# Feed-forward first product as seven block products for blocks 3 to 8, with streamed weights

## The chip, the cores and the metric

The kernel runs on one core of a Trainium2 chip. The metric is the device time of one execution in microseconds (us), taken as the median of several runs. The profiler's trace of one execution lists the instructions of the five engines: TensorE (PE; PEld is its weight load), VectorE (DVE), ScalarE (ACT), GpSimd (POOL) and SyncE (SP), on whose queue all DMAs of this kernel are issued.

## The reference

Three stages over 8 sequences of 576 tokens with 512 features; T = 4608 tokens in all.

```python
# 1 attention with landmarks, per head (8 heads of 64): A, Bm, C are softmax products with 32 means of q and k
out = A @ Z @ C @ v                     # Z: six steps of Z = 2 Z - Z Bm Z
# 2 feed-forward block
u = x + real(fft(fft(x, axis=1), axis=2))
un = (u - mean(u)) / sqrt(var(u) + 1e-6)
x = u + relu(un @ w_ch1) @ w_ch2        # w_ch1 512 x 2048, w_ch2 2048 x 512
# 3 gated block; x_prev is x moved by one token
k = relu((mu_k x + (1 - mu_k) x_prev) @ w_k)     # 512 x 1024
v = k * k @ w_v                                   # 1024 x 512
r = sigmoid((mu_r x + (1 - mu_r) x_prev) @ w_r)   # 512 x 512
return r * v
```

## The kernel before, in words

Every dense product is made with float16 halves. A float32 value is split into a high half and a low half, and a product is the sum of three matmuls (`PARTS`: high with high, high with low, low with high).

The program is recorded first and ordered afterwards. `Plan` collects every operation with a cost, and `issue()` is a list scheduler: on each engine it takes, among the operations that are ready in its own model of time, the one with the largest key. The key is the longest path of costs to the end (`tail`) plus the `lead` under which the operation was recorded: NOW 1000 for operations on the path of a feed-forward block, START 400 for the first sequence, SOON 200 for the later sequences, CONVERT 170 for the conversion of w_ch1 and w_ch2, 0 for the weights of stage 3. The order of each engine and of the SP queue is then fixed in the program. The matmuls of the feed-forward blocks and of stage 3 carry `chain=True`: they run in the order of recording, with a lead of 0, and everything else on TensorE (names with `gp`) goes between them. Where the plan sees TensorE idle for longer than some 0.45 us before the end of block 0 it puts matmuls on zeros into the gap (line 1142: `spare` before the first block, `acc<-zero` inside a block).

Stage 1 is `batch(b)`, once for each of 8 sequences. It leaves u in `ub`, three buffers of 512 tokens. Stage 2 runs over 9 blocks of 512 tokens (blocks 0 to 8): `norm(i)` (lines 1218 to 1285) makes the normalized operand `un`, and `block_a(i)` (lines 1287 to 1331) makes the two products. Its `first(f)`, one for each of 16 column groups of w_ch1, is 12 matmuls of 512 columns into a PSUM bank `ph`, then Relu on ACT and the low half on DVE into `h`. Its `second(f)` is 12 matmuls of 512 columns into the four banks `acc`. Firsts and seconds alternate, each second one step behind.

Weights arrive as 64-bit numbers whose bits the kernel converts itself. `Weights.run` loads a piece of 128 x 512 into a staging buffer, converts it with three operations on ACT and two on DVE, and leaves the two halves in SBUF. Of such pieces w_ch1 has 16 and w_ch2 has 16; both weights stay in SBUF (`w1`, `w2`) for all of stage 2. Staging buffers are two of `wst` and one inside `more`, which lies where the third `ub` buffer will be.

Stage 3 has already the form that the change brings to stage 2: its product with w_k is made in seven products of half-size blocks with matmuls of 256 columns (`Gated.first`, lines 1481 to 1543), with weight sums that `Weights.pair` (lines 576 to 588) makes in the background during blocks 1 to 3 of stage 2, writes to DRAM (`dw_k`) and loads again before stage 3.

Of the kernel before, what the change touches and what calls it, by code (L numbers as in the profile page):

```python
# [28 lines left out]
NB = T // BLK  # L29
HS = S // 2 + 1  # L30
# [112 lines left out]
NOW, START, CONVERT, SOON = 1000.0, 400.0, 170.0, 200.0  # L143
# [381 lines left out]
class Weights:  # L525
# [18 lines left out]
    def single(self, src, top):  # L544
# [3 lines left out]
        st = iss.tile(self.pool, [128, 2 * WCH + 2], I32, "wst", bufs=2)  # L548
# [14 lines left out]
    def pair(self, srcs, dram):  # L563


        iss = self.iss
        v_, s_, g_ = iss.v, iss.s, iss.g
        (a, e0), (b, e1) = [self.single(x, self.tops[0]) for x in srcs]
        h = WCH // 2
        u, w = slice(0, h), slice(h, WCH)  # L570
        s1, s2, s3, s4 = e0[:, u], e0[:, w], e1[:, u], e1[:, w]
        g_.tensor_tensor(s1, a[:, w], b[:, w], op=ALU.add)
        g_.tensor_tensor(s2, s1, a[:, u], op=ALU.subtract)
        g_.tensor_tensor(s3, a[:, u], a[:, w], op=ALU.subtract)
        g_.tensor_tensor(s4, b[:, u], s2, op=ALU.subtract)
        for x, at in ((a[:, u], 0), (b, 1), (e0, 3), (e1, 5)):
            n = wide(x) // h
            both = iss.tile(self.pool, [128, 2, n, h], F16, "wboth", "wtop1")
            xs = x.rearrange("p (n f) -> p n f", n=n)
            s_.activation(both[:, 0], xs, AF.Copy, scale=WS)  # L580
            v_.scalar_tensor_tensor(
                both[:, 1], xs, WS, both[:, 0], op0=ALU.mult, op1=ALU.subtract
            )
            iss.load(dram[:, :, at:at + n], both)

    def run(self, src, hi, lo, room=None):


        iss = self.iss
        v_, s_ = iss.v, iss.s  # L590
        if room is None:
            st = iss.tile(self.pool, [128, 2 * WCH + 2], I32, "wst", bufs=2)
            top = self.tops[self.count % 2 if hi is not None else 0]
            self.count += 1
        else:
            st, top = room
        iss.load(st.bitcast(U8)[:, 1:8 * WCH + 1], src.bitcast(U8))

        def words(dt, at):
            return st.bitcast(dt)[:, at:2 * WCH + at].rearrange("p (f w) -> p f w", w=2)[:, :, 0]  # L600

        x = words(F32, 2)
        byte = st.bitcast(I8)[:, 8:8 * WCH + 8].rearrange("p (f b) -> p f b", b=8)[:, :, 0]
        s_.activation(x, byte, AF.Prelu, bias=self.EDGE, alpha=self.STEEP)
        s_.activation(
            top.bitcast(I8).rearrange("p (f b) -> p f b", b=4)[:, :, 3], x, AF.Prelu,
            scale=8.0, bias=-8.0 * (56.0 + self.EDGE), alpha=1.0 / self.STEEP,
        )  # L610
        v_.scalar_tensor_tensor(
            words(I32, 1), words(I32, 1), 5, top,
            op0=ALU.logical_shift_right, op1=ALU.bitwise_or,
        )
        w = words(F32, 1)
        dram = None
        if hi is None:
            dram = lo
            both = iss.tile(self.pool, [128, 2, WCH], F16, "wboth", "wtop1")
            hi, lo = both[:, 0], both[:, 1]  # L620
        s_.activation(hi, w, AF.Copy, scale=WS)
        v_.scalar_tensor_tensor(lo, w, WS, hi, op0=ALU.mult, op1=ALU.subtract)
        if dram is not None:
            iss.load(dram, both)
# [465 lines left out]
def build(nc, tc, a):  # L1090
# [5 lines left out]
    with stack, tc.manual_schedule():  # L1096
# [51 lines left out]
        w1 = [iss.tile(pa, [128, 4, FF1], F16, f"w1{x}") for x in "hl"]  # L1148
        w2 = [iss.tile(pa, [128, 16, DM], F16, f"w2{x}") for x in "hl"]
        weights = Weights(iss, com)  # L1150

        def piece(name, rows, cols, parts, at):

            r, c = 128 * rows, WCH * cols
            sl = slice(c, c + WCH)
            return (
                a[name][r:r + 128, 2 * c:2 * c + 2 * WCH], parts[0][:, at, sl],
                parts[1][:, at, sl],
            )

        w12_items = []
        for g in range(4):
            w12_items += [piece("w_ch1", c, g, w1, c) for c in range(4)]
            w12_items += [piece("w_ch2", f, 0, w2, f) for f in range(4 * g, 4 * g + 4)]


        shapes = {"w_k": [128, 2, 7, 2, FF2 // 2], "w_v": [128, 2, 8, DM], "w_r": [128, 2, 4, DM]}
        kept = {
            n: iss.dram(tc.dram_tile(x, F16, name="d" + n), x, F16, "d" + n)
            for n, x in shapes.items()  # L1170
        }

        def far(name, rows, cols):
            r, c = 128 * rows, WCH * cols
            return (
                a[name][r:r + 128, 2 * c:2 * c + 2 * WCH], None,
                kept[name][:, :, rows, c:c + WCH],
            )

        def far_pair(name, c, g):  # L1180
            col = 2 * WCH * g
            h = WCH // 2
            return (
                [a[name][128 * r:128 * r + 128, col:col + 2 * WCH] for r in (c, c + 2)],
                kept[name][:, :, :, c, h * g:h * g + h],
# [3 lines left out]
        far_items = [far("w_v", f, 0) for f in range(8)] + [far("w_r", c, 0) for c in range(4)]  # L1189
# [28 lines left out]
        def norm(i):  # L1218
# [13 lines left out]
            uc = [iss.tile(pa, [128, BLK], F32, "uc", f"uc{c}") for c in range(4)]  # L1232
# [42 lines left out]
            rb = spread(r)  # L1275
            un = []
            for c in range(4):
                v_.scalar_tensor_tensor(uc[c], uc[c], 4.0, rb, op0=ALU.mult, op1=ALU.mult)
            iss.lead = NOW
            for c in range(4):  # L1280
                hi, lo = [iss.tile(pa, [128, BLK], F16, "un", f"un{x}{c}") for x in "hl"]
                s_.activation(hi, uc[c], AF.Copy)
                v_.tensor_tensor(lo, uc[c], hi, op=ALU.subtract)
# [3 lines left out]
        def block_a(i, un):  # L1287
            u = ub[i]
            acc = acc_banks()
            hs = {}  # L1290
            iss.lead = NOW

            def first(f):
                ps = ph()
                sl = slice(128 * f, 128 * f + 128)
                for c in range(4):
                    for n, (x, y) in enumerate(PARTS):
                        mm(
                            ps, w1[x][:, c, sl], un[c][y], c == 0 and n == 0,
                            c == 3 and n == 2, chain=True,  # L1300
                        )
                h = hs[f] = iss.tile(com, [128, 2, 512], F16, "h", bufs=3)
                s_.activation(h[:, 0], ps, AF.Relu)
                v_.scalar_tensor_tensor(
                    h[:, 1], ps, 0.0, h[:, 0], op0=ALU.max, op1=ALU.subtract
                )

            def second(f):
                h = hs.pop(f)
                for m in range(4):  # L1310
                    sl = slice(128 * m, 128 * m + 128)
                    for n, (x, y) in enumerate(PARTS):
                        op = mm(
                            acc[m], w2[x][:, f, sl], h[:, y], f == 0 and n == 0,
                            f == 15 and n == 2, chain=True,
# [372 lines left out]
```

## Time and profile before

| | us |
|---|---|
| median of 3 runs | 1493.27 (1493.11 to 1494.37) |
| the profiled execution, its own time | 1494.1 |
| its span from first to last instruction | 1492.3 |
| TensorE busy (share of the span) | 1476.0 (99%) |
| DVE, ACT, POOL busy | 906.2, 619.1, 341.6 |
| start of block 0 (first `ph` matmul) | 69.16 |
| start of stage 3 | 1028.3 |

The blocks of stage 2 start at about 69, 202, 320, 440, 550, 660, 770, 861 and 946 us. Until block 6 the matmuls of the sequences run between those of the blocks; from block 7 on the blocks run alone. Matmuls are pipelined in the engine, so that a duration of 379 ns for 512 columns is longer than the time from one to the next; the pace is read from the chain of waits, which gives the time of a run of matmuls.

### The profile page before, as it was taken

The numbers are of one execution on the slowest core, as the hardware profiler recorded it, in microseconds if no ns is written. First come the engines' busy times: TensorE is split into PE (matmuls) and PEld (weight loads), VectorE is DVE, ScalarE is ACT, GpSimd is POOL, SyncE is SP. The second block draws the span as 40 slices with busy tenths as digits, with TensorE's granted clock in tenths as the row PEclk, the third lists the DMA queues.
The fourth block names the chain that finished last, engine by engine and source line by source line (L and its number), as shares of the span: only waits on it lengthen the run. The fifth ranks groups of instructions, "written<-read, shape, count | busy, mean of one in ns | idle before, by whom it ended". The sixth has DMA issues, their size and how long they took to land.

```text
span 1492.3 us, 23013 instructions
## 1 busy us (share of the span) xinstructions
PE 1476.0 (99%) x9189; PEld 798.9 (54%) x9189; DVE 906.2 (61%) x1830; ACT 619.1 (41%) x1292; POOL 341.6 (23%) x398
## 2 busy tenths in 40 slices
PE   9999999999999999999999999999999999999998
PEld 5554455554554544545544444445656666666664
DVE  7877685766757646535435271212877788768762
ACT  4666544444354432322323131113455545554531
POOL 3002122132301201201202040000442435353410
PEclk9999999999999999999999999999999999999999
DMA  8353241232243311100005000001001001100100
GB/s 291 109 183 118 83 164 38 91 103 85 78 140 104 128 48 50 47 29 0 1 29 212 0 29 1 29 0 57 22 36 57 29 29 57 57 29 32 54 29 29
DMA packets 48987, 101.14 MB, mean 68 GB/s; under 512 B 4336, under 2 KB 14832, under 8 KB 48368
## 3 DMA queue, kind: packets, MB, share of 16 engines
q1 hardware_dynamic: 48880, 99.67, 19.6%
q8 instruction: 72, 1.18, 0.3%
q14 instruction: 35, 0.29, 0.1%
HBM read 73.97 MB, written 25.69 MB: 67 GB/s over the span
## 4 chain that ended last, share of the span: by engine, by line
PE 95%; DVE 2%; ACT 1%; DMA 1%; issue 0%; POOL 0%; DVEq 0%; ACTq 0%; POOLq 0%
PE acc L333 37%; PE ph L333 36%; PE gp L333 18%; PE gp L349 3%; PE spare L1142 1%; DMA dw_k<-wboth 0%; DVE small L188 0%; DMA yb<-ys 0%; PE acc L1142 0%; ACT Y L188 0%; DVE uc L188 0%; DVE bdY L188 0%; DVE bdR L188 0%; DMA out<-o 0%; DVE un L188 0%
## 5 line engine op out<-in xcount | busy, mean ns | idle before, releaser
L333 PE MATMUL ph<-un,w1h 128*128 128x512 f16 x1152 | 352.9, 379 | 0.1
L333 PE MATMUL acc<-h,w2h 128*128 128x512 f16 x1152 | 349.6, 379 | 0.4 <-ACT w2h L188 0.4
L188 DVE SCALAR_TENSOR_TENSOR h<-ph,h 128x512 f16<-128x512 f32 x144 | 99.1, 688 | 217.8 <-ACT h L188 217.0
L333 PE MATMUL ph<-un,w1l 128*128 128x512 f16 x576 | 218.5, 379 | 0.8 <-DVE w1l L188 0.8
L333 PE MATMUL acc<-h,w2l 128*128 128x512 f16 x576 | 218.6, 380 | 0.3 <-DVE w2l L188 0.3
L188 ACT ACTIVATE h<-ph 128x512 f16<-128x512 f32 x144 | 85.8, 596 | 282.0 <-PE ph L333 281.3
L333 PE MATMUL acc<-w_v,k 128*128 128x512 f16 x864 | 199.0, 379 | 0.0
L333 PE MATMUL ph<-xk,w_k 128*128 128x256 f16 x1512 | 183.7, 275 | 3.9 <-ACT xk L188 2.4
L333 PEld LDWEIGHTS <-w2h 128*128 128x128 f16 x1152 | 113.2, 99 | 126.0 <-issue 6.2
L333 PEld LDWEIGHTS <-w1h 128*128 128x128 f16 x1152 | 112.5, 99 | 126.7 <-issue 12.4
L333 PEld LDWEIGHTS <-w_k 128*128 128x128 f16 x1512 | 149.0, 99 | 40.9 <-issue 4.7
L333 PEld LDWEIGHTS <-k 128*128 128x128 f16 x864 | 84.6, 98 | 85.8
L188 POOL TENSOR_TENSOR xk<-xt,xk 128x512 f16<-128x512 f32 x63 | 86.6, 1386 | 130.0 <-ACT xk L188 129.2
L333 PE MATMUL gp<-w_r,xr 128*128 128x512 f16 x432 | 99.3, 379 | 0.3 <-POOL xr L188 0.3
L333 PEld LDWEIGHTS <-w2l 128*128 128x128 f16 x576 | 56.8, 99 | 69.3 <-issue 9.2
L333 PEld LDWEIGHTS <-w1l 128*128 128x128 f16 x576 | 57.2, 99 | 64.7 <-issue 6.3
L188 DVE TENSOR_TENSOR rk<-ph,rk 128x512 f32<-128x512 f32 x54 | 37.2, 689 | 88.9 <-ACT rk L188 62.0
L188 ACT ACTIVATE rk<-ph 128x512 f32<-128x512 f32 x72 | 42.9, 596 | 89.8 <-PE ph L333 81.6
L188 ACT ACTIVATE k<-rk 128x512 f16<-128x512 f32 x72 | 44.8, 627 | 83.4 <-DVE rk L188 83.4
L188 POOL TENSOR_TENSOR sq<-sq 128x513 f32<-128x513 f32 x27 | 37.8, 1399 | 164.7 <-ACT sq L188 164.0
L188 DVE SCALAR_TENSOR_TENSOR rk<-rk 128x512 f32<-128x512 f32 x72 | 71.3, 1004 | 3.2 <-ACT rk L188 2.2
L188 DVE SCALAR_TENSOR_TENSOR xt<-yb,mus,xt 128x512 f32<-128x512 f32 x72 | 60.2, 870 | 13.0 <-POOL xt L188 7.4
(175 smaller groups left out, 1995.9 us busy)
## 6 DMA issues: line engine op xcount, KB each, us to landing
wst<-in_w_ch SPq DMA_DIRECT2D x24, 512.0 KB, 3.8
q<-in_q SPq DMA_DIRECT2D x16, 578.0 KB, 5.7
k<-in_k SPq DMA_DIRECT2D x16, 576.0 KB, 4.9
ys<-ub SPq DMA_DIRECT2D x36, 256.0 KB, 2.1
out<-o SPq DMA_DIRECT2D x36, 256.0 KB, 2.0
yb<-ys SPq DMA_DIRECT2D x8, 1026.0 KB, 5.3
v<-in_v SPq DMA_DIRECT2D x8, 1024.0 KB, 6.9
more<-in_w_ch SPq DMA_DIRECT2D x8, 512.0 KB, 4.5
```

What stands on the lines that cost most here:

```text
L188: f(real(out), *map(real, args), **{k: real(x) for k, x in kw.items()})
L333: self.nc.tensor.matmul(out.real(), lhsT=lhsT.real(), rhs=rhs.real(), start=start, stop=stop, **kw)
L349: self.nc.tensor.transpose(out.real(), in_.real(), ident.real())
L1142: nc.tensor.matmul(into.real() if into else spare[0], lhsT=z.to_broadcast([128, 128]), rhs=z.to_broadcast([128, 512]), start=not into, sto ...
```

## The change

- For blocks 3 to 8 (`NP = 3`) the product un @ w_ch1 is made in seven half-size products (Strassen's scheme in the form with few additions). For each quarter of w_ch1 (512 of its 2048 columns) `Block.first(g)` runs seven products of 12 matmuls of 256 columns instead of four groups of 12 matmuls of 512 columns, and combines them: three copies of a PSUM bank on ACT, three additions on DVE, and four outputs (Relu on ACT, low half on DVE). `operands` makes seven pairs of halves of un with four additions, where `norm` made four pairs.
- Blocks 0 to 2 keep the twelve-matmul groups (`Block.plain`), in quarters, in the order 2, 3, 0, 1. In every block the second product is cut into halves of 6 matmuls and lags by one whole quarter: the last quarter of a block is multiplied during the first quarter of the next block.
- Neither weight stays in SBUF. `convert(g)` converts a quarter for block 0 and writes the halves to DRAM: `w1p` (plain), three of the seven blocks of `w1d`, and `w2d`. Blocks 1 to 8 load each quarter of both weights (w1: 1 MiB plain, 1.75 MiB with seven blocks; w2: 1 MiB). w1 has room for three plain quarters or two of seven blocks, w2 for three quarters.
- `background()` loads w_ch1 a second time, in 8 pairs of pieces, converts them again, makes four of the seven weight blocks of each pair with four subtractions or additions on POOL, splits them and writes them to `w1d`, with lead `SUMS` 200. The weights of stage 3 follow with lead 0, as before.
- `CONVERT` goes from 170 to 400. The staging buffers of the first three quarters are four; those of the last quarter two.
- In stage 3 w_v is loaded in two parts, one of them when the buffers of stage 2 are free; the scratch tiles of the product with w_k are five in the common pool (`rm`) where they were six (`rk`).

```diff
-NOW, START, CONVERT, SOON = 1000.0, 400.0, 170.0, 200.0
+NOW, START, CONVERT, SOON, SUMS = 1000.0, 400.0, 400.0, 200.0, 200.0
+NP = 3
...
-        for x, at in ((a[:, u], 0), (b, 1), (e0, 3), (e1, 5)):
+        for x, at in ((e0, 3), (e1, 5), (a[:, u], 0), (b, 1))[0:2 if sums else 4]:
...
+        w1t = iss.place(pa, [128, 2 * 28 * HB], F16, "w1", "w1")
+        def w1_room(n):
+            x = 28 * HB * (n % 2)
+            return w1t[:, x:x + 28 * HB].rearrange("p (x w c f) -> p x w c f", x=2, w=7, c=2)
...
+        def w2_room():
+            return iss.tile(pa, [128, 2, 4, DM], F16, "w2", bufs=3)
...
+        def operands(both):
...
+            split(0, b11)
+            v_.tensor_tensor(b11, b12, b11, op=ALU.subtract)
+            split(4, b11)
+            split(1, b21)
+            split(2, b22)
+            v_.tensor_tensor(b12, b22, b12, op=ALU.subtract)
+            v_.tensor_tensor(b22, b22, b11, op=ALU.subtract)
+            split(5, b22)
+            split(6, b12)
+            v_.tensor_tensor(b21, b21, b22, op=ALU.subtract)
+            split(3, b21)
...
+        def product(ps, w, x, opens):
+            for f in range(2):
+                for c in range(2):
+                    for n, (y, z) in enumerate(PARTS):
                         mm(
+                            ps[:, HB * f:HB * f + HB], w(y, c, f), x(z, c),
...
+            def first(self, g):
...
+                def out(t, a, z):
...
+                    s_.activation(hi, t, AF.Relu)
+                    v_.scalar_tensor_tensor(lo, t, 0.0, hi, op0=ALU.max, op1=ALU.subtract)
+                px, py = ph(), ph()
+                run(px, 0, 0, True)
+                t1 = copy(px)
+                run(py, 3, 4, True)
+                yield 1
+                run(px, 4, 5, False)
+                t2 = copy(px)
+                yield 2
+                run(px, 5, 6, False)
+                t3 = copy(px)
+                v_.tensor_tensor(t3, py, t3, op=ALU.add)
+                yield 2
+                run(px, 2, 3, False)
+                out(t3, 1, 1)
+                out(px, 1, 0)
+                yield 1
+                run(py, 6, 2, False)
+                v_.tensor_tensor(t2, py, t2, op=ALU.add)
+                out(t2, 0, 1)
+                yield 1
+                pz = ph()
+                run(pz, 1, 1, True)
+                v_.tensor_tensor(t1, pz, t1, op=ALU.add)
+                out(t1, 0, 0)
+                yield 1
...
+        def convert(g):
+            was, iss.lead, iss.slack = iss.lead, CONVERT, 0.6
+            w1, w2 = w1_plain(g), w2_room()
...
+            for c in range(4):
+                weights.run(
+                    rows_of("w_ch1", c, g), sbuf=w1[:, :, c // 2, c % 2],
+                    room=rooms[c] if g < 3 else None,
                 )
+            if NP > 1:
+                iss.load(w1p[g], w1)
+            for x, k, z in ((0, 0, 0), (1, 1, 0), (2, 1, 1)):
+                for y in range(2):
+                    iss.load(w1d[g][:, y, x], w1[:, y, k, :, z])
+            for f in range(4):
+                weights.run(
+                    rows_of("w_ch2", 4 * g + f, 0), sbuf=w2[:, :, f],
+                    room=rooms[f] if g < 3 else None,
+                )
+            iss.load(w2d[g], w2)
...
+        for g in range(3):
+            convert(g)
+        def background():
+            iss.slack = 0.6
+            iss.lead = SUMS
+            for g in range(4):
+                for c in range(2):
+                    weights.pair(
+                        [rows_of("w_ch1", r, g) for r in (c, c + 2)], w1d[g][:, :, :, c], True
+                    )
...
-            block_a(i, norm(i))
+            if i:
+                blocks.append(Block(i, None))
+            block = blocks[i]
+            both = norm(i)
+            block.un = plain_operands(both) if i < NP else operands(both)
+            for g in range(4):
+                if i:
+                    iss.lead = NOW
+                    n = 4 * i + g
+                    block.w1s.append(w1_plain(n) if i < NP else w1_room(n))
+                    iss.load(block.w1s[g], w1p[g] if i < NP else w1d[g])
+                for n in block.plain(g) if i < NP else block.first(g):
+                    for x in late[0:n]:
+                        x()
+                    late = late[n:]
+                if i:
+                    block.w2s.append(w2_room())
+                    iss.load(block.w2s[g], w2d[g])
+                late = block.halves(g)
+                if i == 0 and g == 1:
+                    convert(3)
+                    background()
...
+        for n in ("w_k", "w_r", "w_v0"):
+            fetch(pb, n)
...
+        fetch(pb2, "w_v1")
```

## Rows read from the trace of the kernel before

**Rows 1.** Page: the span, and busy time of each engine (share, instructions).

```profile
span 1492.3 us, 23013 instructions
PE 1476.0 (99%) x9189; PEld 798.9 (54%) x9189; DVE 906.2 (61%) x1830; ACT 619.1 (41%) x1292; POOL 341.6 (23%) x398
```

**Rows 2.** Windows: us, then busy us of PE, PEld, DVE, ACT, POOL; granted clock; DMA share, GB/s.

```profile
0.00:69.16 69.16, 66.19 (x523) 40.07 (x523) 53.50 (x150) 38.56 (x98) 13.95 (x25) 0.95 0.60 212
69.16:200.00 130.84, 127.86 (x813) 63.07 (x813) 98.84 (x229) 82.97 (x176) 19.57 (x24) 1.00 0.39 128
...
290.00:400.00 110.00, 109.74 (x743) 58.16 (x742) 75.30 (x191) 47.77 (x120) 25.32 (x32) 1.00 0.31 95
...
540.00:650.00 110.00, 109.94 (x715) 56.00 (x714) 57.07 (x148) 34.63 (x89) 16.38 (x21) 1.00 0.12 43
...
944.00:1028.40 84.40, 84.40 (x394) 38.29 (x392) 15.21 (x23) 9.55 (x16) 0.00 (x0) 1.00 0.04 15
...
1050.00:1090.00 40.00, 36.48 (x222) 22.23 (x220) 31.20 (x43) 20.18 (x36) 17.65 (x16) 0.93 0.08 27
```

**Rows 3.** Chain of waits, in order: start us, us, what; blocks 7 and 8 and stage 3.

```profile
1005.11 2.59 PE ph L333 x12
...
1114.37 2.62 PE ph L333 x24
```

**Rows 4.** TensorE groups by shape: count, busy us, mean ns of one, idle before and releaser.

```profile
L333 PE MATMUL ph<-xk,w_k 128*128 128x256 f16 x1512 | 183.7, 275 | 3.9 <-ACT xk L188 2.4 <-POOL xk L188 0.9 <-ACT rk L188 0.7
L1142 PE MATMUL acc<-zero 128*128 128x512 f16 x58 | 15.9, 381 | 0.0
```

**Rows 5.** Page, groups: stage 3's product with w_k, its weight loads and evacuation.

```profile
L333 PEld LDWEIGHTS <-w_k 128*128 128x128 f16 x1512 | 149.0, 99 | 40.9 <-issue 4.7
...
L188 DVE TENSOR_TENSOR rk<-ph,rk 128x512 f32<-128x512 f32 x54 | 37.2, 689 | 88.9 <-ACT rk L188 62.0
L188 ACT ACTIVATE rk<-ph 128x512 f32<-128x512 f32 x72 | 42.9, 596 | 89.8 <-PE ph L333 81.6
```

**Rows 6.** Operations on staging buffers: ns min/median/max, first and last start us.

```profile
L188 ACT ACTIVATE wst<-wst x44: 643/667/765, 22.4 to 527.9; 128x512 f32<-128x512 int8 x44
L188 ACT ACTIVATE wtop<-wst x44: 761/782/840, 23.1 to 529.2; 128x512 int8<-128x512 f32 x44
L188 DVE SCALAR_TENSOR_TENSOR wst<-wst,wtop x44: 676/686/1154, 32.1 to 533.0; 128x512 int32<-128x512 int32 x44
L188 ACT ACTIVATE wboth<-wst x28: 423/659/697, 233.7 to 535.6; 128x512 f16<-128x512 f32 x24, 128x256 f16<-128x256 f32 x4
L188 POOL TENSOR_TENSOR wst<-wst x16: 609/842/852, 231.5 to 382.4; 128x256 f32<-128x256 f32 x16
L188 DVE SCALAR_TENSOR_TENSOR w2l<-wst,w2h x12: 677/682/1514, 54.2 to 197.3; 128x512 f16<-128x512 f32 x12
```

**Rows 7.** DMA issues: engine, operation, count, KB each, median us from issue to landing.

```profile
wst<-in_w_k SPq DMA_DIRECT2D x8, 512.0 KB, 4.2
w_k<-dw_k SPq DMA_DIRECT2D x1, 3584.0 KB, 14.7
w_v<-dw_v SPq DMA_DIRECT2D x1, 2048.0 KB, 19.8
dw_k<-wboth SPq DMA_DIRECT2D x12, 256.0 KB, 3.3
```

**Rows 8.** SP queue in order: when those transfers were issued; a parked queue.

```profile
791.71 0.61 SPq L317 DMA_DIRECT2D w_k<-dw_k  x1
794.02 0.46 SPq L317 DMA_DIRECT2D w_v<-dw_v  x1
149.57 35.82 SPq L317 DMA_DIRECT2D wst<-in_w_ch  x6
```

**Rows 9.** DVE in order of time: the last sequence's u.

```profile
790.11 0.82 DVE L188 TENSOR_TENSOR ub<-gp,d 128x287 f32<-128x287 f32 x2 [1.44 <-PE gp L333]
```

**Rows 10.** ACT in order of time: the operand of block 1.

```profile
191.66 0.62 ACT L188 ACTIVATE un<-uc 128x512 f16<-128x512 f32 x1
```

More of the change, by code (lines that the diff above doesn't have):

```diff
@@ L561, in single, with split, top, pair @@
         return self.words(st, F32, 1), self.words(st, F32, 2)
[L563 to L568, printed above, removed]
+    def split(self, x, hi, lo):
+        self.iss.s.activation(hi, x, AF.Copy, scale=WS)
+        self.iss.v.scalar_tensor_tensor(lo, x, WS, hi, op0=ALU.mult, op1=ALU.subtract)
+    def top(self, far):
+        self.count += 1
+        return self.tops[0 if far else self.count % 2]
+    def pair(self, srcs, dram, sums):
+        iss, g_ = self.iss, self.iss.g
+        (a, e0), (b, e1) = [self.single(x, self.top(True)) for x in srcs]
         h = WCH // 2
@@ L579, in pair, with run @@
             xs = x.rearrange("p (n f) -> p n f", n=n)
[L580 to L583, printed above, removed]
+            self.split(xs, both[:, 0], both[:, 1])
             iss.load(dram[:, :, at:at + n], both)
[L586 to L624, printed above, removed]
+    def run(self, src, dram=None, sbuf=None, room=None):
+        w, _ = self.single(src, self.top(sbuf is None), room)
+        if sbuf is not None:
+            if len(sbuf.shape) > 3:
+                w = w.rearrange("p (n f) -> p n f", n=2)
+            self.split(w, sbuf[:, 0], sbuf[:, 1])
+            return
+        both = self.iss.tile(self.pool, [128, 2, WCH], F16, "wboth", "wtop1")
+        self.split(w, both[:, 0], both[:, 1])
+        self.iss.load(dram, both)
 def phase1(a, iss, psum, const, pool, ident, ublock):
@@ L1162, in build @@
[L1162 to L1185, printed above, removed]
+        def rows_of(name, r, g):
+            return a[name][128 * r:128 * r + 128, 2 * WCH * g:2 * WCH * g + 2 * WCH]
+        shapes = {
+            "w_k": [128, 2, 7, 2, FF2 // 2], "w_r": [128, 2, 4, DM],
+            "w_v0": [128, 2, 4, DM], "w_v1": [128, 2, 4, DM],
+        }
@@ L1334, in build @@
-        more = iss.place(pa, [128, 4 * BLK], I32, "more", "ub_2")
-        rooms = [None, None, (
-            more[:, 0:2 * WCH + 2], weights.clear(more[:, 2 * WCH + 2:3 * WCH + 2])
-        )]
-        iss.lead, iss.slack = CONVERT, 0.6
-        for n, x in enumerate(w12_items):
-            weights.run(*x, room=rooms[n % 3] if n < 24 else None)
-        iss.lead = 0.0
-        for x in far_pairs:
-            weights.pair(*x)
-        for x in far_items:
-            weights.run(*x)
-        iss.slack = 0.0
+                if not closes:
+                    return
@@ new lines, in second, with halves @@
+                u = ub[self.i]
+                for m in (2 * half, 2 * half + 1):
+                    v_.scalar_tensor_tensor(
+                        u[m], self.acc[m], 1.0 / (256 * WS), u[m], op0=ALU.mult, op1=ALU.add
+                    )
+                    iss.load(ys[:, m, BLK * self.i:BLK * self.i + BLK], u[m])
+            def halves(self, g):
+                return [
+                    partial(self.second, f, k) for f in ORDER[4 * g:4 * g + 4] for k in range(2)
+                ]
@@ new lines, in build @@
+        for g in range(3):
[7 more added lines that the diff above has]
+                        [rows_of("w_ch1", r, g) for r in (c, c + 2)], w1d[g][:, :, :, c], True
+                    )
+            iss.lead = 0.0
+            for x in far_pairs:
+                weights.pair(*x, False)
+            for x in far_items:
+                weights.run(*x)
+            iss.slack = 0.0
```

218 lines of the change are left out of this document (136 added, 82 removed).

## The prediction, made before the changed kernel was built or run

> **What bounds the kernel now.** I read four views. First the page's busy times: TensorE is busy for 1476.0 of 1492.3 us, DVE for 61%, ACT 41%, POOL 23% [rows 1]. A busy TensorE may only be a pipelined one, so the second view is the chain of waits: in blocks 7 and 8 it is an unbroken alternation of `ph` and `acc` pieces, 2.59 us for 12 matmuls each [rows 3], so 215.8 ns for each matmul of 512 columns. Nothing else enters: TensorE is paid by the column, and the end is set by how many columns it is given. Third, the windows [rows 2]: from 200 us on TensorE is busy in practically all of every stretch, also where sequences still run beside blocks, while DVE has 57 of 110 us there. Work of other engines is hidden, and matmul time taken out of a block is time taken off the end, as long as the operands keep up. Fourth, the matmuls on zeros, which count as busy but are holes: 58 in `acc` [rows 4], at 215.8 ns 12.5 us, all in block 0. That block is not bound by TensorE but by what feeds it: the conversion of the weights, whose last piece of w2 is split at 197.3 us [rows 6], 5 us before the block ends, and the second sequence, whose last operand is made at 191.66 us [rows 10].
>
> **What is removed.** A block's first product is 16 pieces of 2.59 us, 41.4 us. In the new form it is 4 quarters x 7 products x 12 = 336 matmuls of 256 columns. Stage 3 runs this very pattern: 24 of them take 2.62 us [rows 3], 109.2 ns each, so 336 take 36.7 us. The saving is 41.44 - 36.68 = 4.76 us a block, 28.6 us for blocks 3 to 8. It is not 1/8 of the columns (5.2 us), since two short matmuls cost 218.4 ns against one long 215.8. The second products keep their number and size.
>
> **Evacuation of the products.** Each quarter gets three more ACT copies (596 ns) and three more DVE additions (689 ns) [rows 5], about 1.8 and 2.1 us in a quarter of some 19.5 us of TensorE. Their cover is the matmuls put between the products, 6 or 12 of the second product, so 1.3 to 2.6 us for a copy of 0.6 us. DVE, at 57.07 of 110 us where sequences run [rows 2], goes to about 57 + 4 x 2.1 + some 5 for seven operand pairs and four additions, so 70 of 105 us. In stage 3 the same pattern lost TensorE 0.7 us to a copy (ACT rk) in 126 products [rows 4]; for 168 products that is 0.9 us. Bounds 0 and 5 us (0.2 us a quarter); I take +1, the row being the same pattern.
>
> **The operands.** Seven splits replace four at each block start. Only the pair of the first product is needed at once, and a block now starts with its predecessor's last quarter still to be multiplied (10.4 us of matmuls as cover). I cost it at nothing; without cover it would be one split, 1.3 us a block, inside the bound above.
>
> **Start and block 0.** Nothing in the arithmetic of block 0 changes, but its feeding does. CONVERT at 400 lifts the conversions above the second sequence (200). The last quarter has to wait for freed room. Each quarter adds eight stores to the SP queue, at 0.46 to 0.61 us of issue each [rows 8], about 16 to 20 us of queue time in all, and this queue parks in order: one loading of six pieces held it for 35.82 us [rows 8], and behind it stand the loads of the third sequence. For the better end: if conversions are never late the holes vanish, -12.5 us. For the worse: a piece costs ACT 0.667 + 0.782 + 0.66 = 2.1 us [rows 6]; 24 pieces were converted after the block began, 50 us of ACT; if half of that is put in front of the second sequence, block 1's operand comes 25 us later, and the block boundary with it. So -12.5 to +25. ACT had 83 of 131 us busy there and DVE 99 [rows 2], the same sum of work as after the change; what is advanced on one side is delayed on the other. I take +3, near no change, for the stores and the waiting for room.
>
> **Sums in the background.** A pair costs, in order: load 4.2 us [rows 7]; two conversions, 2 x (0.667 + 0.782 + 0.686) = 4.3; four POOL operations of 0.842, 3.4; two splits of 1.34, 2.7 [rows 6]; store 3.3 [rows 7]: about 18 us, and with two staging buffers the next pair can't overlap it. Eight pairs need 143 us at least. They can begin when the staging buffers come free, about 200 us if as late as before, and are due, a quarter before use, from 410 to 490 us (block 3 starts at about 440, its quarters 27 us apart). So the sums fit at up to 36 us a pair. The four pairs for w_k had their POOL work from 231.5 to 382.4 us [rows 6], three intervals of 50 us, at the lowest priority and with four splits and stores each instead of two. I take 0: a pair with half of the splits and a higher lead should run at about 30. Its engines' time is hidden: 34 us of ACT, 22 of DVE and 27 of POOL lie between 200 and 490 us, where DVE has 75.30 of 110 us, ACT 47.77 and POOL 25.32 [rows 2].
>
> **Streams.** Blocks 3 to 8 load 2.75 MiB a quarter, in about 19.5 us where blocks run alone: 148 GB/s. The loads of w_k and w_v moved 5632 KB between 791.71 us and 794.02 + 19.8 = 813.8 us [rows 7, 8], 261 GB/s even without what else ran then. At that rate a quarter takes about 11 us, and each has one quarter of room ahead. In the stretch of 290 to 400 us 95 GB/s are moved besides [rows 2]; there a quarter lasts 27 us, so the sum is about 200. Hidden; the price if not is below.
>
> **Stage 3.** Five scratch tiles instead of six can make a copy wait for an output: 0 to 0.5 us in each of 18 halves, 0 to 9 us; against it the first copy no longer waits for the old buffers, which was 0.7 us [rows 4]. I take +1. The waits for the late operand of its block 1 stay: the stretch from 1050 us holds 3.5 us of holes and a granted clock of 0.93, the only one below 0.99 behind the start [rows 2], so that a longer hole there would also cost clock; w_v's second half is issued beside that operand's load.
>
> **The sum.** -28.6 + 3 + 1 + 0 + 1 = -23.6 us against the profiled execution's 1494.1: 1470.5. The median of the runs lies 0.8 us below that execution: 1469.7, so 1470.
>
> **Rivals.**
> *The starved start.* Block 1 waits for the second sequence, with 15 to 25 us of holes instead of 12.5 and the boundary moved. For it: the priorities are turned round exactly where TensorE already has its only holes [rows 4]. Against it: the conversion ends earlier by as much. At the worse end the start costs +25 in place of +3: 1470 + 22 = 1492; its middle is 1484. Chance 0.16.
> *The dense start.* The holes go, -12.5 in place of +3: about 1455. For it: the lag of a quarter gives slack to every consumer. Chance 0.07.
> *Late sums: slower.* At 50 us a pair, the rate of [rows 6], eight pairs starting at 200 end at 600 us, 110 us after the last is due. The stall is 8r - 290 for r us a pair; it eats the 23.6 us forecast from r = 39 on. At r = 42 it is 46 us, so 1516. The streams act in the same place: a load parked in the SP queue behind a store that waits (35.82 us in [rows 8]) stalls the quarter it feeds, and 0.7 us in each of 32 streamed quarters would also eat the gain. Against both: the priority, half the splits, and a quarter of room ahead. Chance 0.13.
> *Short matmuls bound by weight loads.* A weight load takes 99 ns [rows 5] in a slot of 109.2 ns. If the loads didn't hide, a product matmul would cost 99 + 109 = 208 ns, 336 of them 70 us, 28 us more than now in each of six blocks: about 1640. The row of stage 3 speaks against it: 24 in 2.62 us, sustained [rows 3]. Chance 0.01. The Trainium skill (TensorE: Matmul & The Clock Gate, Back-to-back issue gap) has such a rule: in a stream of load and matmul pairs the spacing is set by both, and it gives 81 ns at 128 columns and 131 ns at 512, by which an estimate for 256 is 98 ns and the change would lose 336 x 98 - 192 x 131 ns = 7.8 us a block; here the rows give 215.8 and 109.2 ns, so the measurement decides against it, and agrees with that section's other formula, columns / 2.4 + 2.5 ns.
> *Nothing gained.* What TensorE gives up in blocks 3 to 6 could be taken back by the sequences, if they set the pace. But the last sequence's u is written at 790.11 us [rows 9], some 70 us before block 7 needs it (861), and the blocks are shortened by only 19 us until then; block 8, with no sequence beside it, gains in any case. That leaves 1490 to 1496. Chance 0.03.
>
> **How the numbers follow.** Forecast (1460 to 1479): 0.60. Range: from 1457, which takes in half of the dense start, to 1491, which takes in nearly all of the starved start: about 8 in 10. Below and above lie the rest of these and the slower rival. What a measurement of this kernel can tell from no change is about 0.2%, 3 us. Faster: 0.60 + 0.16 + 0.07 = 0.83; same 0.03; slower 0.14.
>
> **What would show it.** Right, if the chain of waits in blocks 7 and 8 has 2.62 us for 24 `ph` matmuls between halves of `acc`, and blocks 6 to 8 last about 78 us instead of 83 to 84; if the matmuls on zeros in `acc` stay between 0 and 25 us; if TensorE's waits name no DMA of w1 or w2. Wrong, if TensorE waits at block 3 for `w1d`, if the operand of block 1 comes much after 192 us, or if blocks 3 to 8 show waits of 1 us or more per quarter for `rm`.

## The result, and the profile after

| | before | after |
|---|---|---|
| median of 4 runs each (lowest to highest), us | 1493.37 (1493.11 to 1494.37) | 1466.45 (1465.4 to 1468.58) |
| ratio, with 95% interval | | 0.982 (0.9803 to 0.9837) |
| profiled execution, its span, us | 1494.1, 1492.3 | 1466.6, 1464.8 |
| start of stage 3, us | 1028.3 | 999.4 |

The change makes the kernel 26.9 us faster; the profiled executions differ by 27.5. The forecast was 1470 in a range of 1457 to 1491.

The page of the kernel after, span and busy times, answers to [rows 1]:

```profile
span 1464.8 us, 25189 instructions
PE 1441.8 (98%) x10016; PEld 878.7 (60%) x10016; DVE 995.1 (68%) x1976; ACT 695.9 (48%) x1430; POOL 368.4 (25%) x429
```

TensorE is still the bound. DVE has 89 us more, ACT 77 and POOL 27: second conversions, operand pairs, copies and additions.

The chain of waits (start us, us, what) in block 8 and at the start of stage 3, against [rows 3]:

```profile
910.88 2.62 PE ph L335 x24
...
930.40 2.62 PE ph L335 x24
...
987.70 11.65 PE acc L335 x54
999.36 2.62 PE ph L335 x24
```

24 short matmuls take 2.62 us in block 8 as they did in stage 3, and one quarter follows the other by 19.52 us: a block lasts 78.1 us, where it was 16 firsts and 16 seconds of 2.59 us, 82.9. Behind the last firsts stand the seconds that are left (54 in the row of 11.65 us), and stage 3 begins 28.9 us earlier than before.

TensorE's groups by shape (count | busy us, mean ns | idle before, releaser), then its waits from 200 to 1000 us (us in total, times, longest), all of them:

```profile
L335 PE MATMUL ph<-un,w 128*128 128x256 f16 x2016 | 254.8, 273 | 0.0
L335 PE MATMUL ph<-xk,w_k 128*128 128x256 f16 x1512 | 184.1, 275 | 5.0 <-POOL xk L190 2.2 <-ACT xk L190 2.0 <-ACT rm L190 0.7
```

```profile
PE gp L335 <- DVE bdY L190: 0.4, 1, 0.4
```

The 2016 matmuls of the seven products (6 blocks x 336) never waited by these rows: not for a copy, an operand or a streamed weight. What isn't as clean is the start. Windows of before and after (columns as in [rows 2]); the sums run from 0 to 250 us. Before:

```profile
60.00:110.00 50.00, 49.61 (x357) 27.39 (x357) 39.98 (x112) 32.67 (x74) 2.98 (x6) 0.93 0.49 167
...
sum 250.00, PE 243.87 PEld 132.15 DVE 183.75 ACT 142.39 POOL 47.66; mean PE 40.65 PEld 22.02 DVE 30.62 ACT 23.73 POOL 7.94
```

After:

```profile
60.00:110.00 50.00, 41.48 (x302) 20.29 (x302) 41.23 (x104) 37.74 (x73) 5.45 (x7) 0.90 0.86 293
...
sum 250.00, PE 237.38 PEld 127.47 DVE 185.68 ACT 149.85 POOL 53.48; mean PE 39.56 PEld 21.24 DVE 30.95 ACT 24.97 POOL 8.91
...
70.00:80.00 10.00, 6.49 (x33) 2.35 (x32) 8.12 (x15) 8.21 (x18) 1.06 (x1) 0.72 0.78 221
...
90.00:100.00 10.00, 7.29 (x126) 4.46 (x110) 9.18 (x25) 8.38 (x20) 2.27 (x3) 1.00 0.83 268
```

Up to 250 us TensorE is idle for 12.6 us, where it was 6.1; 8.5 us of them lie between 60 and 110 us, the first third of block 0, where it was 0.4 us. The granted clock there is 0.90 on average, in one slice 0.72. On the other side stand the matmuls on zeros, 17 in `acc` where [rows 4] has 58 (ns min/median/max, first and last start us):

```profile
L1122 PE MATMUL acc<-zero x17: 378/381/390, 181.6 to 188.9; 128*128 128x512 f16 x17
```

The account up to stage 3, with 215.8 ns for a matmul on zeros and a clock below 1 as (1 - clock) x 50 us: zeros -8.8, idle +6.5, clock 5.0 - 3.5 = +1.5, so -0.8 beside -28.6 for the products by their columns, -29.4; the start of stage 3 shows -28.9, and 0.5 us of difference stays open. Stage 3 then lasts 465.4 us, where it was 464.0: +1.4. With the -28.9 that is -27.5, the difference of the spans.

### The profile page after: what moved, and what is told of

It reads as the page before. It is cut to its first block, busy times and chain, and to the rows that moved or that the text cites. A ratio compares the mean times of both kernels' runs of the same rounds, so it can differ in the third digit from the quotient of the medians.

```text
span 1464.8 us, 25189 instructions
## 1 busy us (share of the span) xinstructions
PE 1441.8 (98%) x10016; PEld 878.7 (60%) x10016; DVE 995.1 (68%) x1976; ACT 695.9 (48%) x1430; POOL 368.4 (25%) x429
## 4 chain that ended last, share of the span: by engine, by line
PE 95%; DVE 3%; ACT 1%; DMA 0%; POOL 0%; issue 0%; DVEq 0%; ACTq 0%; POOLq 0%
PE acc L335 38%; PE ph L335 35%; PE gp L335 18%; PE gp L351 3%; PE spare L1122 1%; DVE uc L190 0%; DMA more<-in_w_ch 0%; DVE un L190 0%; DVE small L190 0%; POOL xk L190 0%; DVE A L190 0%; ACT Y L190 0%; DVE mx L190 0%; DVE w L190 0%; DVE cst L190 0%
## 5 line engine op out<-in xcount | busy, mean ns | idle before, releaser
L335 PEld LDWEIGHTS <-w 128*128 128x128 f16 x4320 | 417.7, 99 | 298.7 <-issue 41.7
L335 PE MATMUL acc<-h,w 128*128 128x512 f16 x1728 | 429.2, 380 | 3.3 <-DVE A L190 3.3
L335 PE MATMUL ph<-un,w 128*128 128x256 f16 (+1 forms) x2592 | 405.1, 298 | 3.5 <-DVE un L190 1.9
L190 DVE TENSOR_TENSOR rm<-ph,rm 128x512 f32<-128x512 f32 x126 | 86.9, 689 | 184.9 <-ACT rm L190 130.9
L190 ACT ACTIVATE rm<-ph 128x512 f32<-128x512 f32 x144 | 85.9, 597 | 197.7 <-PE ph L335 196.7
L190 DVE SCALAR_TENSOR_TENSOR h<-ph,h 128x512 f16<-128x512 f32 x72 | 49.4, 686 | 44.0 <-ACT h L190 43.8
L190 DVE SCALAR_TENSOR_TENSOR rm<-rm 128x512 f32<-128x512 f32 x72 | 71.2, 1001 | 3.9 <-ACT rm L190 2.9
L190 POOL TENSOR_TENSOR xr<-xt,xr 128x512 f16<-128x512 f32 x36 | 46.4, 1304 | 81.9 <-ACT xr L190 81.9
L190 DVE SCALAR_TENSOR_TENSOR h<-rm,h 128x512 f16<-128x512 f32 x72 | 53.1, 739 | 10.3 <-ACT h L190 9.7
L190 DVE TENSOR_TENSOR xt<-xt,rs 128x512 f32<-128x512 f32 x72 | 56.7, 828 | 3.0 <-ACT rs L190 2.9
```

The lines of the kernel that those rows point to most:

```text
L190: f(real(out), *map(real, args), **{k: real(x) for k, x in kw.items()})
L335: self.nc.tensor.matmul(out.real(), lhsT=lhsT.real(), rhs=rhs.real(), start=start, stop=stop, **kw)
```

## The experiments

My theory after the result: the products bring what their columns say; the lifted lead of the conversion takes zeros out of block 0; and something else in the restructuring gives as much back as holes at 60 to 110 us. Rivals: that the products bring less and the start more, and, for the holes, the stores, the conversion's own order, late loads, or the lag of a quarter.

**All blocks with plain products.** All else of the change stays: streams, sums, lag, lead.

```diff
-NP = 3
+NP = 9
```

> The changed kernel with all nine blocks in the plain form: streams, background sums (made, stored and then not read), priorities and the lag of a quarter stay; only the seven products of blocks 3 to 8 go. Theory (columns): the gain is the matmul time of six blocks and nothing else, 6 x 4.76 = 28.6 us, so this takes 1466.5 + 28.6 = 1495 us, within 3 us, and has no waits of 1 us or more behind 250 us. Rival (start): part of the gain of 27 us comes from the new feeding of block 0, where the matmuls on zeros went from 58 to 17 (8.8 us); then this stands below the kernel before, at about 1484 to 1487 us. Rival (hidden costs): streams and sums eat time that the products pay for; then seven products gain more than 28.6 us, and this is above 1498 us.

Measured 1494.98 us (1492.74 to 1495.81), ratio to before 1.001 (1.0 to 1.0019). The seven products bring 1494.98 - 1466.45 = 28.5 us; I had 28.6 by columns. The runs of each of the two kernels spread by 3 us, so the agreement to 0.1 us is partly chance. Everything else of the change together is worth little: between nothing and 0.2% of loss by the interval. Its start has the same holes: from 60 to 110 us TensorE is busy for 42.73 us, against 41.48 in after.

**The lead alone, in the kernel before.**

```diff
-NOW, START, CONVERT, SOON = 1000.0, 400.0, 170.0, 200.0
+NOW, START, CONVERT, SOON = 1000.0, 400.0, 400.0, 200.0
```

> The kernel before with one constant of the change: the conversions' lead 400 instead of 170. Theory (columns): the start is bound by the sum of the work of ACT and DVE, so priorities only shift it: 1493.4 within 4 us. Rival (start): the conversions' lead alone removes the matmuls on zeros of block 0, and the time falls by 6 to 12 us, to about 1484. Rival (starved start): the second sequence is pushed behind, block 1's operand comes up to 25 us later than 192 us, and the time rises by 10 to 25 us.

Measured 1487.71 us (1487.63 to 1487.93), ratio 0.9962 (0.9947 to 0.9977): 5.5 us under the kernel before, measured beside it at 1493.23. Its windows and zeros:

```profile
60.00:110.00 50.00, 49.35 (x365) 27.03 (x365) 41.28 (x113) 33.89 (x76) 2.60 (x5) 0.97 0.50 169
...
sum 250.00, PE 245.86 PEld 133.64 DVE 186.93 ACT 142.54 POOL 49.65; mean PE 40.98 PEld 22.27 DVE 31.16 ACT 23.76 POOL 8.28
```

```profile
L1142 PE MATMUL acc<-zero x51: 378/380/390, 94.8 to 191.8; 128*128 128x512 f16 x51
```

Idle 4.1 us instead of 6.1, seven zeros fewer (-1.5), clock 0.97 instead of 0.93 (-2.0): 5.5 us. So the lead is a gain where I feared for the second sequence, and the rest of the restructuring costs 1494.98 - 1487.71 = 7.3 us.

**The change with the old lead.**

```diff
-NOW, START, CONVERT, SOON, SUMS = 1000.0, 400.0, 400.0, 200.0, 200.0
+NOW, START, CONVERT, SOON, SUMS = 1000.0, 400.0, 170.0, 200.0, 200.0
```

> The changed kernel with the conversions' lead back at 170. Theory (columns): 1466.5 within 4 us, the seven products being untouched. Rival (start): the holes of block 0 return (12.5 us of matmuls on zeros instead of 3.7), 1473 to 1478 us. Rival (the lead costs): the holes of the changed kernel between 68 and 101 us, 8 us of waits and a lower granted clock after them, come from conversions that stand before the first operand and the second sequence; with 170 they go and the time falls to 1459 to 1463 us.

Measured 1471.6 us (1466.68 to 1474.36), ratio 0.985 (0.983 to 0.9871), 35 zeros in `acc`. 5 us dearer than the change by the medians, though its lowest run lies among the change's; the same sign and size as the experiment above.

**Seven products from block 2 on.** Block 2 begins at about 310 us, before the sums are through.

```diff
-NP = 3
+NP = 2
```

> The changed kernel with seven products from block 2 on instead of block 3. Theory (columns): one more block gains 4.76 us: 1461.7 us. Rival (late sums): in the changed kernel the eight pairs end at 408.9 us, 28.2 us apart; block 2's last quarter needs the last pair at about 390, with its store and load (4.6 and 7.3 us) before that, so at this rate TensorE waits some 30 us in block 2 and the time is about 1485 to 1492 us. If the higher urgency brings the pairs nearer to their sum of operations (18 us each), the wait goes.

Measured 1469.73 us (1466.26 to 1471.02), ratio 0.9836 (0.9819 to 0.9852): no gain of 4.8 us, for which all runs are too long, but a median 3.3 us above the change, whose interval overlaps this one. TensorE's waits now name a streamed weight:

```profile
PE ph L335 <- DMA w<-dw: 3.2, 1, 3.2
```

With 20 zeros more in `acc` (37, the last at 311.9 us; 4.3 us) that is 7.5 of the 8.1 us between the gain of another 4.8 us and the result. So sums can come too late; the change stays clear of that by where its products start.

**The same with a higher lead for the sums.**

```diff
-NOW, START, CONVERT, SOON, SUMS = 1000.0, 400.0, 400.0, 200.0, 200.0
-NP = 3
+NOW, START, CONVERT, SOON, SUMS = 1000.0, 400.0, 400.0, 200.0, 330.0
+NP = 2
```

> Seven products from block 2 on, and the lead of the sums 330 instead of 200. In the run with block 2 alone added, TensorE lost 3.2 us waiting for a load of the seven-block weights and 20 more matmuls on zeros (4.3 us) near 310 us, against 4.76 us gained. Theory (late sums): with the sums in front of the sequences the pairs come nearer to 18 us each than to 26, those 7.5 us go and the time is 1460 to 1463 us. Rival: the sums push back the sequences that block 2 needs (ACT and DVE are shared), new holes take the place of the old, and it is 1467 us or more.

Measured 1468.39 us (1465.68 to 1468.94), ratio 0.9831 (0.9814 to 0.9847). The wait for the weight falls to 0.5 us, but 40 zeros stand in `acc`. Not told apart from the change, nor from the run before it.

**One room for the streamed w1 instead of two.**

```diff
-            x = 28 * HB * (n % 2)
+            x = 0
```

> The changed kernel with one room instead of two for the seven-block quarters, so that a quarter's load can begin only when the quarter before is used up: the cover of the stream is taken away. Theory (streams are hidden by the quarter of room ahead): each of 24 quarters now waits for a whole load, 7.3 us and its issue, less what matmuls of sequences fill: 100 to 190 us more, so 1570 to 1655 us, with TensorE waiting for the loads of w1. Rival (streams are cheap anyway): under 20 us more.

Measured 1612.75 us in one run, +146.

```profile
PE ph L335 <- DMA w<-dw: 47.9, 21, 6.5
```

```profile
L1122 PE MATMUL acc<-zero x355: 377/381/392, 181.1 to 1114.0; 128*128 128x512 f16 x178
```

355 zeros, 338 more than in the change, are 72.9 us and the waits 47.9. Of the other 25 us the granted clock accounts for nearly all: over the whole span it is 0.979 where the change has 0.994, and (1 - clock) x span is 33 us against 9. It is the quarter of room ahead that hides the streams.

**Each quarter of seven blocks loaded twice.** The second load writes the same bytes.

```diff
                     iss.load(block.w1s[g], w1p[g] if i < NP else w1d[g])
+                    if i >= NP:
+                        iss.load(block.w1s[g], w1d[g])
```

> The changed kernel with each seven-block quarter loaded twice in a row into the same room: 43 MB more, and the second load is issued only when the first has landed, so the SP queue is parked for some 7 us in each quarter. Theory (streams are hidden): two loads take 15 us and still fit in the quarter of 19.5 us that lies ahead; 1466.5 to 1470 us. Rival (streams at their limit): 4.5 MiB a quarter is 242 GB/s where blocks run alone, near the 261 GB/s seen before, and every parked queue delays w2 as well: 2 to 4 us a quarter, 1510 us or more.

Measured 1474.4 us (1474.04 to 1476.26), ratio 0.9877 (0.9863 to 0.9892): +8 us for 44 MB more (24 x 1792 KB). 47 zeros in `acc`, 30 more, are 6.5 us of it, the last at 840 us. My theory had 1470 at most and the rival 1510 or more: the streams are hidden with room to spare, but twice of them isn't free.

**The stores of w1d out of block 0.** The 24 small stores go to block 1, from its loaded quarters.

```diff
-            for x, k, z in ((0, 0, 0), (1, 1, 0), (2, 1, 1)):
-                for y in range(2):
-                    iss.load(w1d[g][:, y, x], w1[:, y, k, :, z])
...
+                if i == 1:
+                    iss.lead = SUMS
+                    for x, k, z in ((0, 0, 0), (1, 1, 0), (2, 1, 1)):
+                        for y in range(2):
+                            iss.load(w1d[g][:, y, x], block.w1s[g][:, y, k, :, z])
+                    iss.lead = NOW
```

> The changed kernel with one part moved: the 24 stores of plain w1 blocks into the seven-block tensor (128 KB each) leave block 0 and are made from the quarters that block 1 loads, with the lead of the sums. Theory (full DMA at the start): in the changed kernel the DMA engines are busy for 0.83 to 1.05 of the time from 80 to 110 us, staging loads land after 6.8 us instead of 4.5, and the in-order ACT and DVE queues then hold the block's operands behind conversions that wait for their load; with the stores gone the waits of TensorE between 68 and 101 us (8 us, and a lower granted clock behind them) shrink by half or more: 1459 to 1463 us. Rival (order): the waits come from the priority of the conversions alone, whatever the loads do: 1466.5 within 1.5 us. Rival (it hits block 1): the stores delay block 1's quarters or hold their room, and the time rises by 2 us or more.

Measured 1467.29 us (1467.19 to 1467.46), ratio 0.9827 (0.9813 to 0.9842). No change: these stores aren't where the holes come from. From 60 to 110 us TensorE is busy for 39.43 us there, less than in the change.

**The operand's multiplications first, a slower model of the DMA, and both.** Holes of after name `un`, and `E` and `A`, the scores of the second sequence (start us, us, engine, line, what [idle before <- releaser]):

```profile
68.84 1.89 PE L335 MATMUL ph<-un,w 128*128 128x512 f16 x8 [0.76 <-DVE un L190]
71.94 0.38 PE L335 MATMUL ph<-un,w 128*128 128x512 f16 x1 [1.21 <-ACT un L190]
...
74.83 0.69 PE L351 MATMUL gp<-ident,E 128*128 128x128 f32 x2 [1.20 <-ACT E L190]
...
100.72 1.89 PE L335 MATMUL acc<-h,w 128*128 128x512 f16 x6 [3.33 <-DVE A L190]
```

In the first I recorded the multiplications of `norm` under NOW; in the second the scheduler's model of a load is made slower; the third has both edits.

```diff
             rb = spread(r)
+            iss.lead = NOW
             for c in range(4):
```

```diff
-                dma = max(dma, end) + op.nbytes / 340e3
-                end = dma + 2.0
+                dma = max(dma, end) + op.nbytes / 300e3
+                end = dma + 4.0
```

> The changed kernel with the four multiplications that finish the normalized operand recorded under the lead of the operand's splits (1000) instead of 400, equal to that of the conversions. Moving the stores out of block 0 had left the time unchanged, so the theory is now: order. The fourth multiplication stood behind three splits on DVE (69.91 us) and its split behind four conversions on ACT (71.28 us), and TensorE waited 4.3 us between 68 and 77 us and ran at a granted clock of 0.72 to 80 us. With the multiplications in front these waits go: 1461 to 1464 us. Rival (late loads): the conversions are late for their loads (ACT waited 1.7 us for one at 65 us), what stands behind them is late in any order, and the time stays at 1466.5 within 1.5 us.

> The changed kernel with one thing changed in the list scheduler's model: a DMA counts 4.0 us of latency and 300 GB/s instead of 2.0 us and 340 GB/s, nearer to what was measured (512 KB of w_ch in 4.5 to 6.8 us, against 3.5 us by the old model, 5.7 by the new). No transfer is added or removed; only the order of the queues is made for later loads. Theory (late loads): conversions no longer stand in front of ready work while their load is under way, and the waits between 60 and 101 us shrink: 1459 to 1464 us. Rival (order by leads alone): 1466.5 within 1.5 us. Rival (a bad plan elsewhere): with loads thought slower the plan leaves room elsewhere, 1470 us or more.

> Both of the last two edits together: multiplications of the operand in front, and the scheduler's model of a DMA at 4.0 us and 300 GB/s. Theory (late loads and order each cost a part of the 8 us of waits between 60 and 101 us): 1457 to 1462 us. If one of them is the whole cause, this equals the better of the two within 1.5 us.

Measured 1472.56 us (1471.2 to 1472.66), 1472.19 (1471.77 to 1474.21) and 1468.02 (1467.51 to 1470.25); ratios 0.9861 (0.9848 to 0.9875), 0.9863 (0.985 to 0.9877) and 0.9839 (0.9826 to 0.9853). None is better than the change, and the first two are some 6 us slower. The holes only move: with the operand first the slice from 100 to 110 us is busy for 6.95 us, with both edits 5.64, and the longest wait becomes one of the second sequence, 8.3 us for `RX`. So neither the operand's place nor the planned time of a load is the cause by itself; in these runs, where one consumer was helped, another was late.

**Half the lag in block 0.** What these kernels share is the recorded order of block 0: a quarter of firsts alone, and its seconds a whole quarter behind. Here they follow by half a quarter, in block 0 only.

```diff
-                for n in block.plain(g) if i < NP else block.first(g):
+                for at, n in enumerate(block.plain(g) if i < NP else block.first(g)):
+                    if i == 0 and at == 3:
+                        late = late + block.halves(g)[0:4]
...
-                late = block.halves(g)
+                late = late + block.halves(g)[4:] if i == 0 else block.halves(g)
```

> The changed kernel, in block 0 alone with a lag of half a quarter instead of a whole one between first and second products: the first two groups of a quarter are multiplied by w2 as soon as they are there. What is open: why the waits of TensorE between 68 and 110 us (8 us, with granted clocks of 0.72 and 0.83) stand in every variant of stores, leads and DMA model, and not in the kernel before. Theory (lag): with a whole quarter of lag block 0 uses up its first eight pieces of w1 within 10.4 us, twice as fast as before, and has nothing else to multiply; with half the lag the waits from 68 to 110 us shrink to 4 us or less and the time falls to 1458 to 1463 us. Rival (a fixed sum): zeros, waits and clock of block 0 together are set by the work of ACT and DVE, which is the same; the holes move to another place, and the time is 1464 to 1469 us.

Measured 1455.59 us (1453.09 to 1458.45), before beside it 1494.03, ratio 0.9748 (0.9735 to 0.9762). This is the best version: 38.4 us under the kernel before and 10.9 us under the change. Its windows, zeros, and the start of stage 3 in its chain:

```profile
60.00:110.00 50.00, 48.12 (x358) 26.37 (x358) 42.50 (x113) 37.09 (x75) 6.60 (x8) 0.97 0.79 281
...
sum 250.00, PE 243.98 PEld 133.16 DVE 187.48 ACT 150.08 POOL 53.23; mean PE 40.66 PEld 22.19 DVE 31.25 ACT 25.01 POOL 8.87
```

```profile
L1122 PE MATMUL acc<-zero x28: 379/380/390, 117.7 to 189.5; 128*128 128x512 f16 x28
```

```profile
989.50 2.62 PE ph L335 x24
```

From 60 to 110 us TensorE is busy for 48.12 us instead of 41.48, with 358 matmuls in place of 302, and the clock is 0.97. DVE and ACT have the same work there within 1.3 us, and the DMAs move no more (281 GB/s, 293 in the change): the engines that feed it do no more work than before, and TensorE has something to multiply meanwhile. The rows of the seconds up to 250 us say which (operation, count: ns min/median/max, first and last start us). The change, then half the lag:

```profile
L335 PE MATMUL acc<-h,w x233: 376/379/631, 91.9 to 249.9; 128*128 128x512 f16 x117
```

```profile
L335 PE MATMUL acc<-h,w x252: 377/379/390, 74.9 to 248.5; 128*128 128x512 f16 x126
```

The first second runs at 74.9 us instead of 91.9 (it was 74.6 in the kernel before), and by 250 us 19 more are done. Against the change: idle to 250 us -6.6, clock -3.5, zeros +2.4, and stage 3 starts 9.9 us earlier; 2.2 us of these I don't place.

The longest hole of the change, 3.33 us before 100.72 us, is of another kind than a late operand. It ends with an operation of the second sequence that reads a PSUM bank:

```profile
100.00 0.67 DVE L190 TENSOR_TENSOR A<-gp,mx 97x512 f32<-97x512 f32 x1
```

In `issue()` a `gp` tile may take any bank that isn't yet in `fixed`, and the four banks of `acc` come into it only when the operands of block 0's first second are ready. In the order that `issue()` plans for this kernel the scores read here lie in the third of these four banks, and the matmuls at 100.72 us are the first to write there. So seconds that start late also leave their banks to the second sequence. A wait of `acc` for `A` stands as well in the runs with plain products (3.3 us), without the stores (5.4), with the operand first (3.0) and with the slower model (4.9), and not in the three kernels whose first second runs at 74 to 75 us: before, the lead alone, half the lag. With the old lead and with both edits, where the seconds start later still, other waits stand in its place. Half the lag changes both things, what TensorE has to multiply and who holds the banks, and no run separates them; the whole lag with `gp` kept out of these banks would.

## Why the prediction was right, step by step

**Products: right.** -28.6 forecast, 28.5 by the experiment with plain products. The pace of a pattern that stage 3 already ran held when it was moved. The Trainium skill's rule on the spacing in a stream of weight loads and matmuls (TensorE: Matmul & The Clock Gate, Back-to-back issue gap), by which six blocks would have lost an estimated 47 us, is contradicted by the same run, and the formula that it gives for a matmul alone, columns / 2.4 + 2.5 ns, comes to the 215.8 and 109.2 ns that were measured.

**Evacuation and operands: right in cause, a little high.** +1 forecast, and no wait for `rm` or `un` in any of the 2016 matmuls. In stage 3 the same pattern lost 0.7 us to a copy; that the cover by seconds is better in a block is the likely reason and wasn't tried.

**Sums: right.** The first and the last of the eight pairs' last stores on SP, then the first load of seven-block weights and the first matmul on them:

```profile
211.34 0.64 SPq L319 DMA_DIRECT2D dw<-wboth  x1
...
408.86 0.59 SPq L319 DMA_DIRECT2D dw<-wboth  x1
```

```profile
393.72 1.85 SPq L319 DMA_DIRECT2D w<-dw  x2
```

```profile
427.98 2.62 PE ph L335 x24
```

Seven intervals in 197.5 us are 28.2 us a pair, where I took about 30 and put the turn at 39. Pairs come due by quarters, so the first loads are issued before the last pair is stored. Block 3 starts 12 us earlier than I had, and the margin is thin: one block earlier TensorE waited 3.2 us for such a load.

**Streams: right, with the reason.** The issues (KB each, median us to landing), against [rows 7]:

```profile
w<-dw SPq DMA_DIRECT2D x24, 1792.0 KB, 7.3
w<-dw SPq DMA_DIRECT2D x32, 1024.0 KB, 8.8
```

Both weights of a quarter land in 16.1 us even one after the other, in a quarter of 19.5, and the room of one quarter stands ahead.

**Start: the mis-sized term.** I took +3 in -12.5 to +25, and it came to about -0.3, by two effects of opposite sign that I hadn't separated. That their sum came so near my +3 was luck. The lifted lead was worth -5.5, measured in the kernel before; the rest of the restructuring cost 7.3. I had taken its gain and its harm as one sum of work, delayed here by as much as advanced there; but the operand of block 1 wasn't delayed, 191.48 us against [rows 10]:

```profile
191.48 0.63 ACT L190 ACTIVATE un<-uc 128x512 f16<-128x512 f32 x1 [1.64 <-DVE uc L190]
```

The step that was wrong is in the rival of the dense start: "the lag of a quarter gives slack to every consumer". In blocks with a full predecessor it does. Block 0 has none: four groups of firsts are 10.4 us of matmuls, and after them, until the next quarter's firsts, nothing else of the block may run, so that each hitch of an operand, a weight or the second sequence is a hole: its first second came at 91.9 us. Half the lag gave back 10.9 us; how much of that is work to fill the holes and how much the banks stays open. I had priced the stores at 16 to 20 us of queue time as well (32 issues of 0.46 to 0.61 us are 15 to 20); without the 24 small ones in block 0 nothing changed.

**Stage 3: right in size, wrong in cause.** +1 forecast, +1.4 measured. But the scratch tiles, on which I had put it, cost 0.7 us as before (`rm` in the row of after, `rk` in [rows 4]); `xk` by POOL went from 0.9 to 2.2. The kernel with plain products has the same 2.2 us and the kernel before with the lead alone 1.0, so it is neither the products nor the lead; why POOL is later I didn't try. And 0.93 isn't the only granted clock below 0.99 behind the start, as I had it: the last stretch of the kernel before, from 1470 us, has 0.96.

**Nothing gained: excluded.** Stage 3 starts 28.9 us earlier, so the sequences took nothing back.

## What to carry to other kernels

A pattern that already runs in the kernel prices its copy elsewhere to a few tenths of a per cent; the uncertain part of such a change is what it does to the start. A software lag between producer and consumer is slack only where an earlier block fills it: give the first block a shorter one. When helping one consumer only moves the holes, look at the order in which the bound engine's own work was recorded, and not at a further feeder.

## What the runs showed of the hardware

Short holes of TensorE went with a lower clock. In after the slice from 70 to 80 us has 3.5 us of holes and a granted clock of 0.72, so part of it ran at 1.2 in place of 2.4 GHz. Over 60 to 110 us the kernels with 8.5 and 7.3 us of holes (after, plain products) had 0.90 and 0.86, those with 1.9 and 0.6 (half lag, lead alone) 0.97. It isn't a simple measure: the kernel before had 0.93 with 0.4 us of holes there, all of it lost from 60 to 70 us.

Loads took longer while the DMA engines were busier. In the window from 10 to 20 us of after they read as full, at 390 GB/s:

```profile
10.00:20.00 10.00, 10.00 (x115) 7.38 (x114) 7.78 (x21) 3.43 (x13) 1.23 (x2) 1.00 1.05 390
```

```profile
wst<-in_w_ch SPq DMA_DIRECT2D x36, 512.0 KB, 4.5
...
more<-in_w_ch SPq DMA_DIRECT2D x12, 512.0 KB, 6.8
```

The same 512 KB land in 4.5 us through `wst` and in 6.8 through `more`, which is loaded at the start alone (14 to 107 us). In that stretch `wst` takes 5.5 us too, and 4.5 from 200 to 600 us; that the full engines are the reason is argued, not tried. The Trainium skill (DMA: Bandwidth & Descriptors, Specifications) gives about 358 GB/s as a core's limit, half of what it states for the memory that two cores share; here, with one core at work, 390 were moved.
